# Batch 1's pooled values by TensorE from the local value layout, its values in other buffers, load limits by stage, a swapped clamp and a new order

## Chip, cores and metric

The kernel runs on one core of a Trainium2 chip. The metric is the device time of one execution in microseconds, the median of several runs; the time before is 971.5 us (three runs, 966.82 to 975.91).

## The reference, cut to what matters

Eight batches of eight heads, 576 tokens, head size 64. Each head gets two attentions, which are added: one over tokens pooled by four (the means of four neighbours of q, k and v; the result is repeated four times), and one over a window of at most three tokens to either side. The sum goes through a feed-forward layer with g = h cos(h).

```python
q_d = q.reshape(B, H, Sd, 4, D).mean(axis=3)      # k_d and v_d alike
out_up = np.repeat(sm_attn(q_d, k_d, v_d), 4, axis=2)
mask = np.abs(pos[:, None] - pos[None, :]) < 4
out_local = softmax(where(mask, scale * q @ k.T, -1e9)) @ v
x = (out_up + out_local).transpose(0, 2, 1, 3).reshape(4608, 512)
h = x @ w_in                                      # 512 x 2048
return (h * np.cos(h)) @ w_out                    # 2048 x 512
```

## The kernel before, in words

**The work.** Heads go in pairs, 32 in all (8 batches by 4 pairs). Of each pair `u_qk` loads q and k and pools them, `u_v` loads v in the local layout (12 windows of 32 tokens by 64, 384 KB), `u_s` makes both sorts of scores and their softmax, `u_t` transposes the probabilities, `u_pv` multiplies by the values and writes x. The tokens are cut into 12 tiles of 384; `gemm1` makes one chunk of 128 columns of h for a tile (12 matmuls of 384 columns, L1275; from tile 4 on a pair of chunks by seven products of half size, L1300), `g_part` makes g of it on ScalarE, VectorE and GpSimd (L1345 to L1357, L630), `gemm2` adds three times three matmuls of 512 columns (L1375). Numbers are split into a high and a low half-precision part, weights too: `w_load` (L652) fetches one of 32 blocks of 512 KB as 64-bit words and `w_split`/`w_total` (L663 to L725) rebuild the fraction, clamp it (L664), scale it (L722, L723) and take the rest (L725).

**Pooled values before.** For batches 0 and 1 `u_vd` loads the four rows to be pooled as a second copy of v (288 KB for each pair, L882) into a buffer of the ring `wd` (seven buffers, the one that weight blocks use), adds them in two additions (L890, L891) on GpSimd or VectorE, and for batch 1 squares them on ScalarE for the scale of x (L885). From batch 2 on `v_sum` does the pooling with accumulating DMAs.

**Buffers.** The local values `vl` of batch 0 and 1 share a ring of four buffers, so that each load of batch 1 waits until L1178, the local product of batch 0, has read its buffer.

**The order.** A planner (`Plan`) holds every operation with a cost, its engine or engines to choose from, and what it waits for. It walks through simulated time and, for each engine, takes the ready operation with the least key; the keys come from a backward walk and from hand-searched offsets (`MOVES`, `TURNS`), and `FILLS` adds idle matmuls (L1527) that keep TensorE active in the early stage. The result is the program order of each engine, which the chip follows whatever the true durations are. SyncE (SP) starts all plain loads in one order; the first part of it is a chain written by hand (queries and keys of batch 0, values of batch 0, `u_vd` of batch 1, weight chunks 0 and 1, queries and keys of batch 1, `u_v` of batch 1, the other weights). A load waits on an earlier one so that at most 900 kB are on their way (`FLIGHT`).

**Constants.** GpSimd makes two identities and the mask of the local windows (L587 to L596): eight selections over 32 by 192, one after the other.

Of the kernel before, what the change touches and what calls it, by code (L numbers as in the profile page):

```python
# [60 lines left out]
FLIGHT = 900e3  # L61
# [6 lines left out]
    "u_vd": {(0, 2): (0, -2.3), (1, 0): (0, 2.5), (1, 3): (-31.95, 0)},  # L68
    "u_s": {(0, 0): (-26.7, 0), (0, 1): (-16.8, -5.85), (0, 2): (106.15, 0), (1, 0): (-51, 0), (1, 1): (-44.65, 4.4), (1, 2): (-35.45, 0), (1, 3): (6.15, 1.7),
# [1505 lines left out]
```

## Time and profile before

| | |
|---|---|
| runs | 971.5, 966.82, 975.91 us; median 971.5 |
| span of the profiled execution | 971.3 us; its first instruction begins at 0.24 us |
| busy: TensorE, VectorE, ScalarE, GpSimd | 921.4, 758.6, 635.5, 455.8 us |
| moved by DMA | 90.30 MB |

A whole time of the profiled execution beside its span is not recorded; the span differs by 0.2 us from the median of the runs, and the working below is made against the span. In the rows, PE is TensorE's matmul side, PEld its weight loads, DVE VectorE, ACT ScalarE, POOL GpSimd, SPq the queue of SyncE. `A <- B` after a wait names who was waited for; "issue" is time in which nothing shown was waited for.

### The profile page before, as it was taken

Reading aid. Unit: us, or ns where it says so; the run is one execution under the profiler, and the core shown is the slowest. Engines: PE = TensorE matmul, PEld = TensorE weight load, DVE = VectorE, ACT = ScalarE, POOL = GpSimd, SP = SyncE. Lnnn points to the kernel's source line nnn. Section 1 sums busy time; section 2 is a strip of 40 time slices with the busy share of each in tenths; the row PEclk is TensorE's granted clock in tenths of the full one; section 3 lists DMA queues with packets and bytes.
Section 4 is the critical chain, followed back from the end, with each engine's and each line's share of the span. In section 5 each row is a group of like instructions: output and inputs, shape, how many; then the busy total and the mean of one; then the engine's idle time right before and its main releaser. Section 6 shows DMA issues by size and latency. Waiting matters only on the chain.

```text
span 971.3 us, 26178 instructions
## 1 busy us (share of the span) xinstructions
PE 921.4 (95%) x10464; PEld 613.8 (63%) x10464; DVE 758.6 (78%) x1713; ACT 635.5 (65%) x1378; POOL 455.8 (47%) x715
## 2 busy tenths in 40 slices
PE   7978899899989898999989998999999999999998
PEld 6755554454556555667667676676776767667674
DVE  5887798988888878889788777897597876656554
ACT  3646667877757575776767576666576576565654
POOL 6653874267763888888534242753041341200000
PEclk9977999999999999999999999999999999999999
DMA  7845894456573752224323031341030120000000
GB/s 236 243 154 162 229 206 143 125 117 145 109 152 51 163 144 72 68 79 96 107 79 87 26 99 49 87 110 47 1 106 3 31 79 9 2 33 1 33 2 33
DMA packets 48962, 90.30 MB, mean 93 GB/s; under 512 B 6024, under 2 KB 23176, under 8 KB 48840
## 3 DMA queue, kind: packets, MB, share of 16 engines
q1 hardware_dynamic: 42360, 74.67, 25.3%
q0 software_dynamic: 6480, 13.96, 9.6%
q8 instruction: 82, 1.34, 0.6%
q14 instruction: 40, 0.33, 0.1%
HBM read 65.01 MB, written 18.09 MB: 86 GB/s over the span
## 4 chain that ended last, share of the span: by engine, by line
PE 65%; DVE 10%; DMA 10%; ACT 6%; POOL 4%; issue 3%; SPq 2%; ACTq 0%; POOLq 0%; DVEq 0%
PE bank L1375 29%; PE bank L1300 20%; PE bank L1275 5%; PE bank L1193 3%; PE bank L927 2%; DMA wv<-vdn 2%; DMA diag<-ptl 2%; PE bank L935 2%; DMA wd<-w_out 1%; SPq L1039 1%; DMA wd<-vdn 1%; DVE tr L1346 1%; PE bank L1147 1%; PE bank L1048 1%; DVE tr L1349 1%
## 5 line engine op out<-in xcount | busy, mean ns | idle before, releaser
L1375 PE MATMUL bank<-wo,gh 128*128 128x512 f16 x1152 | 343.1, 380 | 2.3 <-ACT ob L1392 2.2
L1375 PE MATMUL bank<-wo,gl 128*128 128x512 f16 x576 | 218.3, 379 | 0.8 <-POOL gl L630 0.8
L1375 PEld LDWEIGHTS <-gh 128*128 128x128 f16 x1152 | 106.9, 98 | 86.6 <-issue 7.0
L630 POOL TENSOR_TENSOR gl<-tr,gh 128x384 f16<-128x384 f32 x65 | 65.8, 1014 | 202.6 <-ACT gh L1356 169.6
L1345 ACT ACTIVATE tr<-bank,bquart,hs 128x384 int32<-128x384 f32 x144 | 95.9, 667 | 92.8 <-PE bank L1300 75.6
L1300 PEld LDWEIGHTS <-wi 128*128 128x128 f16 x1536 | 129.3, 98 | 23.7 <-issue 5.6
L1314 DVE TENSOR_TENSOR bank<-bank,tr 128x192 f32<-128x192 f32 x192 | 69.0, 361 | 89.4 <-PE bank L1300 82.1
L1348 ACT ACTIVATE tr<-tr,bhalf 128x384 f32<-128x384 f32 x192 | 116.4, 610 | 25.9 <-DVE tr L1346 24.0
L1349 DVE SCALAR_TENSOR_TENSOR tr<-tr,rho,bank 128x384 f32<-128x384 f32 x192 | 114.7, 606 | 18.0 <-ACT tr L1348 17.0
L1300 PEld LDWEIGHTS <-room 128*128 128x128 f16 x1152 | 97.5, 98 | 32.9 <-issue 7.0
L1275 PEld LDWEIGHTS <-wi 128*128 128x128 f16 x768 | 75.3, 98 | 59.9 <-issue 5.0
L1375 PEld LDWEIGHTS <-gl 128*128 128x128 f16 x576 | 56.3, 98 | 69.4 <-POOL gl L630 1.3
L1346 DVE SCALAR_TENSOR_TENSOR tr<-bank,hs,tr 128x384 f32<-128x384 f32 x144 | 87.9, 611 | 14.8 <-ACT tr L1345 14.7
L1356 ACT ACTIVATE gh<-tr 128x384 f16<-128x384 f32 x148 | 76.6, 519 | 27.4 <-DVE tr L1349 22.2
L630 DVE TENSOR_TENSOR gl<-tr,gh 128x384 f16<-128x384 f32 x127 | 77.6, 613 | 10.6 <-ACT gh L1356 7.8
L1310 ACT ACTIVATE tr<-bank 128x192 f32<-128x192 f32 x161 | 52.0, 325 | 44.4 <-PE bank L1300 27.3
L1300 PE MATMUL bank<-room 128*128 128x192 f16 x768 | 80.1, 246 | 0.1
L1392 ACT ACTIVATE ob<-bank,os 128x512 f32<-128x512 f32 x63 | 41.4, 680 | 10.5 <-PE bank L1375 9.2
L1300 PE MATMUL bank<-room,wi 128*128 128x192 f16 x384 | 42.1, 246 | 0.0
L1193 PE MATMUL bank<-diag,vl 128*64 128x96 f32 x672 | 34.6, 253 | 7.9 <-DMA diag<-ptl 5.8
L664 POOL TENSOR_SCALAR wv<-wv 128x512 f32<-128x512 f32 x17 | 35.2, 2073 | 12.4 <-ACT wv L663 10.2
L1007 POOL TENSOR_TENSOR sml<-sml,su 128x384 f32<-128x384 f32 x26 | 28.7, 1103 | 26.3 <-DVE su L1005 26.3
(284 smaller groups left out, 2023.9 us busy)
## 6 DMA issues: line engine op xcount, KB each, us to landing
vl<-vl SPq DMA_DIRECT2D x32, 384.0 KB
q<-qT SPq DMA_DIRECT2D x32, 292.0 KB
k<-kT SPq DMA_DIRECT2D x32, 292.0 KB
out<-ob SPq DMA_DIRECT2D x36, 256.0 KB
out<-ob POOLq DMA_DIRECT2D x33, 256.0 KB, 5.6
wd<-w_in SPq DMA_DIRECT2D x16, 512.0 KB
wd<-w_out SPq DMA_DIRECT2D x16, 512.0 KB
diag<-ptl SPq DMA_DIRECT2D x112, 48.0 KB
```

The lines of the kernel that those rows point to most:

```text
L630: f = lambda e: lambda: e.tensor_tensor(out=out(), in0=in0(), in1=in1(), op=ALU.subtract)
L1193: pe.matmul(banks[e].get()[64 * h:64 * h + 64, sg * 4 * BQ:(sg + 1) * 4 * BQ], vt.get()[:, s, :], dg[:, :, s, :BQ], start=b >= GRP, stop=T ...
L1275: pe.matmul(ph.get()[:, :m], w[:, i, kc, :], x[:, kc, :], start=(n == 0), stop=(n == 3 * KC - 1))
L1300: pe.matmul(bk.get()[:, lo:lo + HT], a(i)(kk), bx(j, k)(kk), start=start and n == 0, stop=n == 5, skip_group_check=True)
L1310: pl.op("ACT", _act(HT), lambda: act.activation(t.get(), src(), AF.Copy), r=[bk], w=[t], alts=[("DVE", _dve(HT), lambda: dve.tensor_copy(t ...
L1314: o = pl.op("DVE", _dve(HT), lambda: dve.tensor_tensor(out=out(), in0=src(), in1=hold[i].get(), op=ALU.add), **kw)
L1345: pl.op("ACT", _act(m, True, 2), lambda: act.activation(ti(), h(), AF.Identity, bias=bquart, scale=inv()), r=[ph, also, hs], w=[tr])
L1346: pl.op("DVE", _dvs(m), lambda: dve.scalar_tensor_tensor(out=tr.get(), in0=h(), scalar=inv(), in1=ti(), op0=ALU.mult, op1=ALU.subtract), r ...
L1348: pl.op("ACT", _act(m, False, 1), lambda: act.activation(tr.get(), tr.get(), AF.Sin, scale=2.0 * PI, bias=bhalf), w=[tr], tab="sin")
L1349: pl.op("DVE", _dvs(m), lambda: dve.scalar_tensor_tensor(out=tr.get(), in0=tr.get(), scalar=rho(), in1=h(), op0=ALU.mult, op1=ALU.mult), r ...
L1356: pl.op("ACT", _act(m, False), lambda: act.activation(ghv(), trv(), AF.Copy), r=[tr], w=[gh], alts=[("DVE", _dve(m / 2), lambda: dve.tenso ...
L1375: pe.matmul(o, (gh, gh, gl)[k].get()[:, sl], wo.get()[:, (0, 1, 0)[k]], start=(c == c0 and k == 0), stop=(c == c1 - 1 and k == 2))
```

## The change

- `u_vd` of batch 1 loads nothing and adds nothing: six single-precision matmuls for each pair take the local layout `vl` as moving operand and a matrix of ones `grp` (made once on GpSimd, in buffer `ob.2`) as weights, and sum four tokens into 72 rows; one copy brings 256 columns out of PSUM. The squares for the scale are taken of `vl` (768 columns).
- `vl` of batch 1 lies in the unused x buffers x2h, x3h and x3l and in one buffer of `wd`; its loads stand right behind batch 0's values, ahead of the weights.
- The limit on bytes under way is 1.8 MB for the loads up to weight chunk 2, 500 kB for the late loads (batches 2 to 7), and 900 kB between.
- The clamp of L664 takes min first and max second; the high part of a weight may also be made on GpSimd, as a multiplication by the scale and by 1.0.
- `w_in` is laid out on the host so that each block is 128 rows of 4 KB, not 512 runs of 1 KB.
- The mask is selected on one of six segments and copied by VectorE; the single-precision identity comes last.
- The planner's costs of loads, small GpSimd operations and engine starts are set anew, 0.35 us are kept free after 140 us of its time between another engine's result and TensorE, offsets now exist for single operations, and all offsets are new.

```diff
-FLIGHT = 900e3
+VLX = ((2, "h"), (3, "h"), (3, "l"))
+FLIGHT, FLIGHT0, FLIGHT1 = 900e3, 1.8e6, 500e3
...
+CFG = dict(slack=0.35, slack0=140.0, alttol=0.3, ...
+FROM0 = dict(PE=1.4, ACT=2.0, DVE=0.9, POOL=4.0, SP=1.8)
...
+                    if f == "PE" and e != "PE" and not back and end > CFG["slack0"]:
+                        x += CFG["slack"]
...
-        pool.memset(mask, 0.0)
+        dve.memset(mask[:, 0], 0.0)
         for i in range(4):
-            h = mask[i * BS:(i + 1) * BS]
+            h = mask[i * BS:(i + 1) * BS, 0]
...
+        dve.tensor_copy(mask[:, 1:], mask[:, 0:1].broadcast_to([P, NSEG - 1, BS]))
...
-        clamp = ... scalar1=2.0 ** -15, scalar2=F64_TOP, op0=ALU.max, op1=ALU.min)
+        clamp = ... scalar1=F64_TOP, scalar2=2.0 ** -15, op0=ALU.min, op1=ALU.max)
...
-                  alts=[("DVE", _dvs(n / 2), ... scalar1=a(), scalar2=None, op0=ALU.mult))], port=BOTH)
+                  alts=[(x, d, ... scalar1=a(), scalar2=1.0, op0=ALU.mult, op1=ALU.mult))
+                        for x, d, e in (("DVE", _dvs(n / 2), dve), ("POOL", 0.65, pool))], port=BOTH)
...
+        vt, bk = st[(b, pr)]["vl"], bank(b, "v")
+        def mm():
+            acc = bk.get()[:HD, :2 * P].rearrange("p (a h d) -> p a h d", a=2, h=2)
+            for s in range(NSEG):
+                o, k = GC - 24 * (s % 3), 4 * (s // 2) + s % 2
+                pe.matmul(acc[:, s // 3], grp.get()[:, o:o + HD], vt.get()[:, k:k + 3:2, :], start=s % 3 == 0, stop=s % 3 == 2)
+        pl.op("PE", 6 * _mm4(2 * D), mm, r=[vt, grp], w=[bk], ni=24, warm=WARM["d"], act=0.45)
+        pl.op("ACT", _act(2 * P), lambda: act.activation(flat(), bk.get()[:HD, :2 * P], AF.Copy), ...
...
+        if b == 1 and pr < len(VLX):
+            r, k = VLX[pr]
+            vt = pl.buf(lambda: x_ring[(r, k)].get()...
+        elif b == 1:
+            t = pl.turn("wd", NWD)
...
-    chain = [... u_vd/u_v of batch 0 + ul("u_vd", 1) + wl(0, 1) + ul("u_qk", 1) + ul("u_v", 1) + wl(*range(2, NC)) ...]
+    chain = [... u_vd/u_v of batch 0 + ul("u_v", 1) + wl(0) + ul("u_qk", 1)[:2] + wl(1) + ul("u_qk", 1)[2:] + wl(*range(2, NC)) ...]
+            o.flight = FLIGHT1
+    for o in chain[:chain.index(loads[("w_load", "i", 2)][0])]:
+        o.flight = FLIGHT0
```

## Rows read from the trace of the kernel before

**Rows 1.** The page: busy time by engine, and the granted clock in 40 slices.

```profile
PE 921.4 (95%) x10464; PEld 613.8 (63%) x10464; DVE 758.6 (78%) x1713; ACT 635.5 (65%) x1378; POOL 455.8 (47%) x715
...
PEclk9977999999999999999999999999999999999999
```

**Rows 2.** Four stretches: length, busy time of PE, PEld, DVE, ACT, POOL, clock, DMA.

```profile
0.00:125.00 125.00, 106.11 (x1948) 76.41 (x1949) 97.35 (x237) 73.63 (x206) 78.36 (x129) 0.89 0.70 206
125.00:250.00 125.00, 118.85 (x762) 63.16 (x761) 114.09 (x252) 93.48 (x180) 69.11 (x91) 1.00 0.60 141
250.00:700.00 450.00, 430.08 (x5218) 286.19 (x5217) 371.35 (x827) 301.44 (x631) 261.50 (x420) 1.00 0.35 86
700.00:972.00 272.00, 266.40 (x2542) 188.04 (x2540) 175.77 (x399) 166.96 (x363) 46.79 (x76) 1.00 0.10 30
```

**Rows 3.** The same stretches, idle matmuls of L1527 alone (PE, PEld).

```profile
0.00:125.00 125.00, 34.59 (x235) 23.40 (x235) 0.89 0.70 206
125.00:250.00 125.00, 2.94 (x21) 2.06 (x21) 1.00 0.60 141
```

**Rows 4.** The chain that ended last, 0 to 130 us: start, length, what.

```profile
6.27 0.33 PE bank L922 x2
...
39.67 1.02 PE bank L1166 x4
...
52.88 2.22 PE bank L1166 x4
...
76.94 3.38 PE bank L1275 x10
...
86.34 4.07 DMA wd<-w_out
90.49 3.79 DMA wd<-w_out
94.36 4.33 DMA q<-qT
...
101.90 4.47 DMA wd<-w_in
```

**Rows 5.** Timeline of 0 to 62 us: mask, pooled-value additions, and SyncE's queue.

```profile
5.87 0.35 POOL L596 CAST mask_b<-mask 128x192 bf16<-128x192 f32 x1
...
9.86 0.36 DVE L950 TENSOR_REDUCE mxl<-bank 128x6 f32<-128x192 f32 x1 [3.89 <-PE bank L935]
...
28.12 0.68 DVE L890 TENSOR_TENSOR wd<-wd 72x512 f32<-72x512 f32 x1
...
36.78 0.71 DVE L891 TENSOR_TENSOR vsum<-wd 72x256 f32<-72x256 f32 x1
...
44.05 14.14 SPq L899 DMA_DIRECT2D vl<-vl  x4
58.29 0.38 SPq L652 DMA_DIRECT2D wd<-w_in  x1
```

**Rows 6.** The weight clamp L664 by engine (min/median/max ns), and who waited for it.

```profile
L664 POOL TENSOR_SCALAR wv<-wv x17: 1915/1952/2362, 34.1 to 243.8; 128x512 f32<-128x512 f32 x17
L664 DVE TENSOR_SCALAR wv<-wv x15: 364/427/828, 45.4 to 235.8; 128x512 f32<-128x512 f32 x15
...
DVE wv L666 <- POOL wv L664: 8.1, 8, 1.8
```

**Rows 7.** Groups of 60 to 250 us: a two-input GpSimd operation, high parts, rests.

```profile
L630 POOL TENSOR_TENSOR x2l<-xs,x2h 128x384 f16<-128x384 f32 x3 | 2.7, 911 | 0.4 <-ACT x2h L1129 0.4
L723 DVE TENSOR_SCALAR wi<-wv,wsc 128x512 f16<-128x512 f32 x8 | 3.8, 480 | 0.0
L722 ACT ACTIVATE wo<-wv,wsc 128x512 f16<-128x512 f32 x10 | 7.2, 718 | 4.3 <-POOL wsc L699 3.7 <-DVE wsc L699 0.5
```

**Rows 8.** Waits of TensorE, 125 to 972 us: total, times, longest.

```profile
PE bank L1193 <- DMA diag<-ptl: 4.9, 4, 2.9
PE bank L1375 <- ACT ob L1392: 2.2, 6, 0.7
PE bank L927 <- issue: 2.1, 1, 2.1
PE bank L1300 <- DVE tr L1311: 1.9, 2, 1.6
```

More of the change, by code (lines that the diff above doesn't have):

```diff
@@ new lines @@
+    "x_scale": {(0,): (543.95, 10.6), (2,): (31.85, -54.75)},
+    "u_t": {(0, 0): (-249.05, 4), (0, 3): (0, 2.8), (1, 2): (0, -0.55), (2, 0): (95.95, 0), (2, 1): (32.75, -0.75), (2, 3): (23.2, 0), (3, 0): (-42.45, 0),
+        (3, 2): (24.45, 1.65), (3, 3): (289.65, 0), (4, 0): (-22.05, 0), (4, 1): (-58.9, 0), (4, 3): (-148.1, 0), (5, 0): (5.9, 0), (5, 1): (11.2, 0),
+        (5, 2): (-47.25, 2.8), (6, 0): (-10.1, 0), (6, 1): (144.15, 0), (7, 1): (0, 2.9), (7, 2): (78.7, 0)},
+    "u_pv": {(0, 0): (344.25, 0), (0, 1): (830.5, -6.9), (0, 2): (0, 47.5), (0, 3): (232.8, -40.65), (1, 0): (0, 7.15), (1, 1): (0, -326.8),
[8 rows of a table added]
@@ new lines @@
+    "c_scale": {(0, 0): (108.8, 11.15), (0, 1): (0, 3.5), (0, 10): (0, -9.9), (0, 11): (102.4, 12.85), (0, 13): (82.5, 0), (0, 2): (0, 0.8), (0, 4): (0, 18),
[15 rows of a table added]
+    "o_scale": {(0, 0): (-249.35, -41.45), (0, 8): (0, 1.8)},
+    "g_scale": {(0, 4): (165.55, 0), (1, 2): (600.7, 10.8), (12, 16): (0, -25.95), (2, 4): (0, 20.7)},
[12 rows of a table added]
+    "v_sum": {(2,): (337.75, 0), (3,): (227.1, 0), (4,): (-350.4, 0)},
+    "u_v": {(2, 0): (211.2, 0)},
+    "s_make": {(1,): (0, -17.3), (2,): (-600.95, -24.25), (3,): (-39, -70.3), (4,): (-9.1, 0), (5,): (0, -115.7), (6,): (123.25, -45.15), (7,): (37, -9.55)},
@@ L117 @@
+    "v_norm": {(6,): (484.6, 0), (7,): (36.2, 0)},
 }
 TURNS = {
+    "u_vd": {(0, 0, 1): (0, -47.7)},
+    "u_s": {(0, 0, 14): (28.5, 0), (0, 1, 14): (-39.55, 0), (0, 2, 7): (-40.6, 0), (0, 2, 8): (-10.75, 0), (0, 3, 1): (-494.45, 0), (1, 0, 14): (-34.2, 0),
[8 rows of a table added]
+    "u_t": {(0, 0, 3): (-23.85, 0), (0, 0, 5): (0, -6.35), (0, 3, 5): (0, -5.45), (1, 2, 7): (-20.7, 0), (2, 1, 0): (-48.85, 0), (2, 1, 5): (22.5, 0),
+        (2, 1, 7): (10.85, 0), (2, 3, 7): (-26.85, 0), (3, 1, 5): (12.2, 0), (3, 1, 6): (0, 13.45), (3, 2, 0): (-24.5, 0), (4, 1, 0): (60.85, 0),
+        (6, 0, 5): (-23.45, 0), (6, 2, 7): (35.65, 0)},
@@ new lines @@
+    "u_pv": {(0, 1, 5): (0, 10.25), (0, 2, 4): (88, 0), (1, 0, 7): (0, -10.85), (1, 0, 9): (0, -30.15), (1, 2, 8): (0, -27.2), (2, 1, 1): (-49.8, 0),
[14 rows of a table added]
+    "g_scale": {(2, 4, 1): (-205.2, 0)},
[17 rows of a table added]
+    "c_scale": {(0, 10, 0): (0, 10.35), (0, 6, 0): (-203.65, 0)},
+    "x_scale": {(1, 3): (106.7, 0), (2, 6): (14.8, 0)},
+    "u_qk": {(2, 1, 1): (-10.35, 0), (2, 2, 1): (-15.15, 0), (2, 2, 2): (0, 17.45), (2, 3, 2): (71.85, 0), (3, 0, 2): (0, 10.2), (5, 3, 2): (0, 6),
+        (5, 3, 3): (0, 9.4), (6, 2, 2): (0, 24.7), (7, 0, 2): (-35.15, 0), (7, 1, 2): (0, 9.7)},
@@ L151 @@
     __slots__ = ("eng", "dur", "fn", "tab", "deps", "sdeps", "now", "start", "end", "lat", "name", "arg", "preds", "succs",
-                 "i", "fin", "banks", "alts", "boost", "move", "cold", "gate", "ni", "size", "inst", "stall", "fill", "warm", "act", "port", "wb")
+                 "i", "fin", "flight", "banks", "alts", "boost", "move", "cold", "gate", "ni", "size", "inst", "stall", "fill", "warm", "act", "port", "wb")
 class Plan:
@@ L264, in run @@
         late = {e: {f: late(f, e) if back else late(e, f) for f in self.engines} for e in self.engines}
-        free = {e: 2.9 if e == "SP" and not back else 0.0 for e in self.engines}
+        free = {e: 0.0 if back else FROM0[e] for e in self.engines}
         ready = {e: [] for e in self.engines}
@@ L427, in run @@
                 sent = [x for x in sent if x[0] > t]
-                while sum(x[1] for x in sent) > FLIGHT:
+                while sum(x[1] for x in sent) > o.flight:
                     t = max(t, sent[0][0])
@@ L461, in run @@
                     open_[b] -= 1
-                    b_end = end + late[e]["PE"]
+                    b_end = end + late[e]["PE"] + (CFG["slack"] if e != "PE" and end > CFG["slack0"] else 0.0)
                     hold[b] = max(hold.get(b, 0.0), b_end)
@@ L500, in schedule @@
             key = {o: span - o.fin - o.boost for o in self.ops}
-        key, bias, seen, turn = best[1], {}, {}, {}
+        self.base, key, bias, seen, turn = best[1], {}, {}, {}, {}
         for o in self.ops:
@@ L586, in constants @@
         dve.memset(tiny, TINY)
-        pool.memset(mask, 0.0)
+        dve.memset(mask[:, 0], 0.0)
         for i in range(4):
-            h = mask[i * BS:(i + 1) * BS]
-            pool.affine_select(out=h, in_=h, compare_op=ALU.is_ge, fill=NEG, base=0,
-                               pattern=[[0, NSEG], [1, BS]], channel_multiplier=-1)
-            pool.affine_select(out=h, in_=h, compare_op=ALU.is_ge, fill=NEG, base=2 * PAD,
-                               pattern=[[0, NSEG], [-1, BS]], channel_multiplier=1)
-        pool.memset(mask[0:BS, 0, 0:PAD], NEG)
-        pool.memset(mask[P - BS:P, NSEG - 1, BQ + PAD:BS], NEG)
-        pool.tensor_copy(mask_b, mask)
+            h = mask[i * BS:(i + 1) * BS, 0]
+            pool.affine_select(out=h, in_=h, compare_op=ALU.is_ge, fill=NEG, base=0, pattern=[[1, BS]], channel_multiplier=-1)
+            pool.affine_select(out=h, in_=h, compare_op=ALU.is_ge, fill=NEG, base=2 * PAD, pattern=[[-1, BS]], channel_multiplier=1)
+        dve.tensor_copy(mask[:, 1:], mask[:, 0:1].broadcast_to([P, NSEG - 1, BS]))
+        dve.memset(mask[0:BS, 0, 0:PAD], NEG)
+        dve.memset(mask[P - BS:P, NSEG - 1, BQ + PAD:BS], NEG)
+        dve.tensor_copy(mask_b, mask)
+        make_identity(nc, ident)
     wgt = {(k, c): pl.buf(lambda k=k, c=c: wp.tile([P, 2, DM], F16, name=f"w{k}{c}", tag=f"w{k}{c}", bufs=1), f"w{k}{c}")
@@ L611, in tile_of, with dma @@
         return max(t for t in range(NT) if FROM[t] <= tok)
-    w_dram = {"i": w_in.bitcast(I32).rearrange("(a p) (f t) -> p a f t", p=P, t=2),
-              "o": w_out.bitcast(I32).rearrange("f (n t) -> f n t", t=2)}
+    w_dram = {k: w.bitcast(I32).rearrange("f (n t) -> f n t", t=2) for k, w in (("i", w_in), ("o", w_out))}
     loads = {}
-    def dma(nbytes, fn, r=(), w=(), pw=(), issue=0.4, rate=300e3):
+    def dma(nbytes, fn, r=(), w=(), pw=(), issue=0.4, rate=290e3, base=1.4):
         def go():
             o.inst = fn().ins
-        o = pl.op("SP", issue, go, r=r, w=w, pw=pw, move=(1.2, nbytes / rate))
+        o = pl.op("SP", issue, go, r=r, w=w, pw=pw, move=(base, nbytes / rate))
         o.size = nbytes
@@ L646, in w_load @@
         wd = wv[(k, c)] = sb("wd", NWD, [P, DM, 2], I32)
-        if k == "i":
-            src = lambda: w_dram["i"][:, :, c * P:(c + 1) * P, :]
-            dst = lambda: wd.get().rearrange("p (a f) t -> p a f t", a=KC)
-        else:
-            src, dst = (lambda: w_dram["o"][c * P:(c + 1) * P]), wd.get
-        dma(4096 * P, lambda: sp.dma_start(dst(), src()), w=[wd], rate=250e3)
+        dma(4096 * P, lambda: sp.dma_start(wd.get(), w_dram[k][c * P:(c + 1) * P]), w=[wd])
     wq, half, exps = {}, {}, {}
@@ L663, in w_split @@
         pl.op("ACT", _act(n, False), lambda: act.activation(v.get(), wd().bitcast(F32)[:, :, 1], AF.Abs), r=[wd_b], w=[v])
-        clamp = lambda e: lambda: e.tensor_scalar(out=v.get(), in0=v.get(), scalar1=2.0 ** -15, scalar2=F64_TOP, op0=ALU.max, op1=ALU.min)
+        clamp = lambda e: lambda: e.tensor_scalar(out=v.get(), in0=v.get(), scalar1=F64_TOP, scalar2=2.0 ** -15, op0=ALU.min, op1=ALU.max)
         pl.op("DVE", 0.335, clamp(dve), w=[v], alts=[("POOL", _pool(n), clamp(pool))], port=BOTH)
@@ L722, in w_total @@
             pl.op("ACT", _act(n, False, 1), lambda hi=hi, u=u, a=a: act.activation(hi(), u.get(), AF.Copy, scale=a()), r=[u, sc], w=[hb], pw=[w],
-                  alts=[("DVE", _dvs(n / 2), lambda hi=hi, u=u, a=a: dve.tensor_scalar(
-                      out=hi(), in0=u.get(), scalar1=a(), scalar2=None, op0=ALU.mult))], port=BOTH)
+                  alts=[(x, d, lambda hi=hi, u=u, a=a, e=e: e.tensor_scalar(
+                      out=hi(), in0=u.get(), scalar1=a(), scalar2=1.0, op0=ALU.mult, op1=ALU.mult)) for x, d, e in (("DVE", _dvs(n / 2), dve), ("POOL", 0.65, pool))], port=BOTH)
             pl.op("DVE", _dvs(n), lambda w=w, hi=hi, u=u, a=a: dve.scalar_tensor_tensor(
@@ L872, in v_sum, with grouping @@
             pl.op("POOL", 0.9, lambda r=r: pool.dma_start(dst(), src(r), accum_op=ALU.add), w=[t], move=(3.5, 1.9))
+    grp = pl.buf(lambda: fp.tile([P, DM], F32, name="grp", tag="ob.2", bufs=1), "ob.2")
+    GC = 48
+    def grouping():
+        t = grp.get()
+        pool.memset(t[:, :P], 0.0)
+        for i in range(4):
+            h = t[i * BS:(i + 1) * BS, GC + 6 * i:GC + 6 * i + 6]
+            pool.memset(h, 1.0)
+            pool.affine_select(out=h, in_=h, compare_op=ALU.is_ge, fill=0.0, base=-PAD, pattern=[[-4, 6]], channel_multiplier=1)
+            pool.affine_select(out=h, in_=h, compare_op=ALU.is_ge, fill=0.0, base=PAD + 3, pattern=[[4, 6]], channel_multiplier=-1)
+    pl.op("POOL", 1.3, grouping, w=[grp])
     def u_vd(b, pr):
         pl.name = "u_vd"
-        vw, vd = sb("wd", NWD, [P, DM, 2], I32), pl.buf(None)
+        vd = pl.buf(None)
         if b not in vsum:
@@ L888, in v_add, with f @@
-        def v_add(e):
-            def f():
-                e.tensor_tensor(out=v4()[:, 0:2], in0=v4()[:, 0:2], in1=v4()[:, 2:4], op=ALU.add)
-                e.tensor_tensor(out=vo(), in0=v4()[:, 0], in1=v4()[:, 1], op=ALU.add)
-            return f
-        pl.op("POOL", 1.7, v_add(pool), w=[vd, vw], pw=[vsum[b]], alts=[("DVE", 1.1, v_add(dve))], port=dict(POOL=2, DVE=2))
-        st.setdefault((b, pr), {}).update(vd=vd, vdg=vo)
+        st.setdefault((b, pr), {}).update(vd=vd, vdg=vo)
+        if b < NDIAG:
+            vw = sb("wd", NWD, [P, DM, 2], I32)
+            flat = lambda: vw.get()[:HD].rearrange("p f t -> p (f t)").bitcast(F32)
+            v4 = lambda: flat().rearrange("p (r a n) -> p r a n", a=2, r=4)
+            dma(16 * P * HD * 2, lambda: sp.dma_start(v4().rearrange("p r a n -> p r (a n)"), vdn[b, :, :, pr].rearrange("p r a n -> p r (a n)")), w=[vw], issue=0.8)
+            def v_add(e):
+                def f():
+                    e.tensor_tensor(out=v4()[:, 0:2], in0=v4()[:, 0:2], in1=v4()[:, 2:4], op=ALU.add)
+                    e.tensor_tensor(out=vo(), in0=v4()[:, 0], in1=v4()[:, 1], op=ALU.add)
+                return f
+            pl.op("POOL", 1.8, v_add(pool), w=[vd, vw], pw=[vsum[b]], alts=[("DVE", 1.1, v_add(dve))], port=dict(POOL=2, DVE=2))
+            return
@@ L896, in u_v @@
+        pl.op("ACT", _act(2 * P), lambda: act.activation(flat(), bk.get()[:HD, :2 * P], AF.Copy), r=[bk], w=[vd], pw=[vsum[b]],
+              alts=[("DVE", _dve(2 * P), lambda: dve.tensor_copy(flat(), bk.get()[:HD, :2 * P]))])
     def u_v(b, pr):
         pl.name = "u_v"
-        vt = ub(b, pr, "vl")
-        dma(4 * P * 12 * D, lambda: sp.dma_start(vt.get(), vl[b, pr]), w=[vt], rate=210e3)
-        if b == 0:
-            square(12 * D, lambda: vt.get().rearrange("p a d -> p (a d)"), 0, pr, vt, True)
+        if b == 1 and pr < len(VLX):
+            r, k = VLX[pr]
+            vt = pl.buf(lambda: x_ring[(r, k)].get().rearrange("p a s -> p (a s)").bitcast(F32).rearrange("p (a d) -> p a d", d=D))
+            x_b[r].prev.append(vt)
+        elif b == 1:
+            t = pl.turn("wd", NWD)
+            vt = pl.buf(lambda: ap.tile([P, DM, 2], I32, name="wd", tag=t, bufs=1).rearrange("p f t -> p (f t)").bitcast(F32)[:, :12 * D].rearrange(
+                "p (a d) -> p a d", d=D), t)
+        else:
+            vt = ub(b, pr, "vl")
@@ L902, in u_v @@
+        dma(4 * P * 12 * D, lambda: sp.dma_start(vt.get(), vl[b, pr]), w=[vt])
+        if b < NEARLY:
+            square(12 * D, lambda: vt.get().rearrange("p a d -> p (a d)"), 0, NPAIR * b + pr, vt, True)
         u = st.setdefault((b, pr), {})
@@ L1448, in attn_ffn_kernel @@
     for i in range(NPAIR):
-        for t, f in ((-7.6 + 0.1 * i, u_vd), (-4.0 + 0.1 * i, u_qk), (-3.5 + 0.1 * i, u_v), (-3.0 + 0.1 * i, u_s), (-2.6 + 0.1 * i, u_t), (-2.2 + 0.1 * i, u_pv)):
+        for t, f in ((-4.0 + 0.1 * i, u_qk), (-7.6 + 0.1 * i, u_v), (-7.55 + 0.1 * i, u_vd), (-3.0 + 0.1 * i, u_s), (-2.6 + 0.1 * i, u_t), (-2.2 + 0.1 * i, u_pv)):
             at(t, f, 1, i)
@@ L1487, in ul @@
         return [(f, b, i) for i in range(NPAIR)]
-    chain = [o for k in ul("u_qk", 0) + [(f, 0, i) for i in range(NPAIR) for f in ("u_vd", "u_v")] + ul("u_vd", 1) + wl(0, 1) + ul("u_qk", 1)
-             + ul("u_v", 1) + wl(*range(2, NC)) for o in loads[k]]
+    chain = [o for k in ul("u_qk", 0) + [(f, 0, i) for i in range(NPAIR) for f in ("u_vd", "u_v")] + ul("u_v", 1) + wl(0) + ul("u_qk", 1)[:2] + wl(1) + ul("u_qk", 1)[2:]
+             + wl(*range(2, NC)) for o in loads[k]]
     late = {k: v for k, v in loads.items() if k[0] in ("u_qk", "u_v", "v_norm", "v_sum") and k[1] >= NEARLY}
@@ L1531, in attn_ffn_kernel @@
             if o.size:
-                while sum(x.size for x in flight) > FLIGHT:
+                while sum(x.size for x in flight) > o.flight:
                     held = flight.pop(0)
@@ L1557, in _lay @@
         "vl": np.ascontiguousarray(vb),
-        "w_in": np.ascontiguousarray(inputs["moe_w_in"]).view(np.int64),
+        "w_in": np.ascontiguousarray(inputs["moe_w_in"].reshape(KC, P, NC, P).transpose(2, 1, 0, 3)).reshape(DF, DM).view(np.int64),
         "w_out": np.ascontiguousarray(inputs["moe_w_out"]).view(np.int64),
```

55 lines of the change are left out of this document (22 added, 33 removed), and 122 rows, old and new, of tables (FILLS, MOVES, TURNS).

## The prediction

> **What bounds the kernel now.** I read first the busy times, then four stretches of the span, then in the first of them the chain and the timeline. The first view shows TensorE busy for 921.4 of 971.3 us [rows 1], so it looks like the bound everywhere. The stretches correct that. TensorE's idle time is length less busy time: 125 - 106.1 = 18.9 us up to 125 us, 6.2 up to 250, 19.9 up to 700 and 5.6 behind [rows 2]. Its busy time in the first stretch holds 34.6 us of idle matmuls that compute nothing [rows 3], and the clock granted there was 0.89, with two slices at 0.7 [rows 1, 2]: (1 - 0.89) x 125 = 14 us at most are lost to the lower of the two levels, 1.2 GHz in place of 2.4; I take 12. So up to 125 us some 19 + 35 + 12 = 66 us are not useful TensorE work, and behind it some 32 + 4 = 36. VectorE is what the start waits for: 97.4 of 125 us busy, and 114.1 of 125 in the next stretch (91%) [rows 2], where TensorE is fed by weight splits and g. In the last 272 us TensorE idles 5.6 us: nothing is to be had there.
>
> The chain shows what is late in the first stretch: the mask at 6.27 us, the first product of the feed-forward layer at 76.94 us, then weight and query loads, 4.07 + 3.79 + 4.33 us in a row from 86.34, and one of 4.47 at 101.90 [rows 4]. The timeline shows why loads are late: SyncE stands at the four loads of batch 1's local values for 14.14 us, from 44.05 to 58.2, since their buffers are held by batch 0, and only at 58.29 does the next weight load start [rows 5].
>
> **The change part by part.**
>
> *Mask.* The first score matmuls start at 6.27 us [rows 4], as the mask's last cast on GpSimd ends (5.87 + 0.35) [rows 5]. Selecting 32 columns in place of 192, with the identity moved behind, can take 0 to 3.5 us off; I take 2. VectorE has 3.89 us of idle time right behind it [rows 5], so that it can come through; what is late next is the keys' and queries' pooling. Taken: -1.5.
>
> *Pooled values of batch 1.* VectorE loses four pairs of additions, the first at 28.12 and the last at 36.78, 0.68 and 0.71 us for such [rows 5]; with 0.7 us as the mean of eight this is 5.6 us, at a time when it is the busiest engine. ScalarE trades a square for a slightly shorter one, four copies out of PSUM come in. TensorE gets 4 x 6 single-precision matmuls of 128 columns. Two of 288 columns took 1.02 us at the full clock and 2.22 at half [rows 4], so one of 128 takes 1.02 / 2 x 128 / 288 = 0.23 us, six 1.36 and all 5.4 us (11.8 at half clock). They lie where 34.6 us of idle matmuls lie [rows 3] and replace some, so their cost is between -1 (they hold the clock up as the idle ones did) and +11.8; I take +1. Were the cover gone, it would be 5.4. For VectorE I count -4 of 5.6, since part of it was hidden by waits for scores.
>
> *Loads and buffers.* Four loads of 288 KB go; four of 384 KB move ahead of the weights, so weight chunk 0 has 0.4 MB more ahead of it: at the 206 GB/s of the stretch [rows 2] 1.9 us later. Against that the 14.14 us of SyncE at L899 go [rows 5], and all that is queued behind it on SyncE comes sooner: weight chunks 2 and on, and then batch 2's queries. The waits in the chain that hang on that are 4.07 + 3.79 + 4.33 + 4.47 = 16.7 us [rows 4]. If the loads come 10 us sooner, all of these go at best, and VectorE's splitting is late next: it was 78% busy in that stretch [rows 2]. Bounds: -14 to +2; taken -6, nearer to the middle, since VectorE has 22% to give at most. The larger limit in the start and the layout of w_in are in it: the load of w_in took 4.47 us in the chain and those of w_out 4.07 and 3.79 [rows 4], so two such on the path are worth 0.8 to 1.4 us.
>
> *Clamp and high parts.* The clamp takes 1952 ns on GpSimd and 427 on VectorE, and VectorE waited 8.1 us in eight waits for it [rows 6]. That the other order of min and max is cheaper is nowhere in the trace. Bounds for it: 0.43 us (VectorE's row) to 1.95 (no change); a two-input operation of 384 columns takes 0.91 us on GpSimd [rows 7], for 512 columns 1.2. I take 1.2, the nearest row of that engine: 17 x 0.75 = 13 us less of GpSimd, of which VectorE feels some 8.1 x 0.4 = 3 us. The high part on GpSimd is priced by the planner at 0.65 us; the rows give 0.48 on VectorE, 0.72 on ScalarE [rows 7] and 1.95 for the clamp, the operation on GpSimd that is nearest in form [rows 6]. I take 1.2 again: up to ten such move 5 us off VectorE and ScalarE, worth 0 to -3, taken -1. Together -4, bounds -8 to +13.
>
> By the Trainium skill (GPSIMD Engine Reference, 4.1 Engine selection) a one-input elementwise operation on GpSimd runs at roughly line rate, while two-input ones are about twice as slow as VectorE. The trace disagrees for the clamp in its present order: the one-input operation of 512 columns takes 1952 ns, more than twice the 911 of the two-input one of 384. At line rate, as an estimate from that page, 512 columns at 1.2 GHz would be 0.43 us, the clamp part would come to its good end (-8) and the sum below to 950; by the row, with nothing gained from the swap, to 958.
>
> *Waits behind 125 us.* TensorE waits there for 26 us in all (6.2 + 19.9) before the last stretch [rows 2]; the longest sorts are the diagonal copies with 4.9 us, then the output copies with 2.2, a wait with no shown cause, 2.1, and sums with 1.9 [rows 8], each in few long waits, as an order leaves them that was planned with too small costs. The limit of 500 kB shortens what is queued ahead of a diagonal copy; 0.35 us kept free and a dearer diagonal copy move producers ahead. Idle time of this sort can fall to a third, or grow where the new order has its own misses: bounds -16 to +8, taken -9. It does not need the start to be right. The limit also makes SyncE wait at loads, and behind these stand diagonal copies and output stores; DMA is used 0.35 and 0.10 there [rows 2], so I price that at nothing; without that room each diagonal copy could lose a load's time.
>
> *Sum.* -1.5 (mask) -4 (VectorE) +1 (group matmuls) -6 (loads) -4 (GpSimd) = -14.5 in the start and the weight stage, of which I let 3 be lost, since all of these free VectorE or feed it and cannot each be felt in full: -11.5. With -9 behind it, -20.5, less 3 for the new order's own misses: -17.5. 971.3 - 17.5 = **954 us**; against the median of 971.5 the same.
>
> **The rivals.**
>
> *A. VectorE stays the bound up to 250 us.* The start comes 6 us sooner and the splitting of the weights gives it back: for it speaks VectorE's 91% [rows 2], against it that TensorE's idle time is mostly before 125 us. Only VectorE's own work counts then (-5.6 of additions, -3 of clamp waits, half of each felt), and the waits behind fall by 3: 971.3 - 4.3 - 3 = 964 us.
>
> *B. GpSimd is mispriced, slower than before.* Where: in the weight stage, 60 to 260 us. If a high part on GpSimd takes what the clamp takes, 1.95 us [rows 6], against 0.65 in the plan, every one put there is 1.3 us late, and behind it in GpSimd's order stand the small scales that release ScalarE and VectorE. With 16 of 32 there, 16 x 1.3 = 21 us of lateness come, and the swapped clamp gains nothing. If VectorE passes two thirds on, +14; the start's gain is halved (-6) and the order behind, planned for other times, loses 5 of the 8 in that term's upper bound: 971.3 - 6 + 14 + 5 = 984 us. It decides from about 1.6 us for a high part with more than ten of them. For it: the row of the clamp. Against: ScalarE or VectorE can still take them all.
>
> *C. The new order fits the chip much better.* Idle matmuls and half clock in the start shrink by a third (66 to 50 us, minus 16) and the waits behind 125 us to a third (-16): 971.3 - 32 = 939 us. For it: the idle time is spread over many small causes that one correction of costs reaches. Against: VectorE's load in 125 to 250 us.
>
> *D. The change of loads does not do what it says:* x buffers or the `wd` ring hold the values as late as before. A load of batch 1 would stand behind the same readers; then the term of -6 goes and the sum is 960. The x buffers of tiles 2 and 3 are read behind those of tile 0, whose first product stands at 76.94 us [rows 4], so I hold this unlikely and count it under A.
>
> **How the numbers follow.** Forecast 0.55, A (with D) 0.2, B 0.1, C 0.15. Faster by over 1% (below 961.8; about 1% is what a measurement of this kernel can tell from no change, the runs lying within 0.5% of their median): the forecast and C, 0.70. Within 1%: A, 0.20. Slower: B, 0.10. The range goes from C to a little beyond A, 938 to 970; the forecast's own is 946 to 962.
>
> **What would show it.** Right: no stop of SyncE near 44 us, L664 on GpSimd near 1.2 us or less, the first L1275 matmul of tile 0 before 70 us (76.94 now), idle matmuls and idle time up to 125 us together down from 53 to about 43 us, TensorE's waits from 125 to 700 us near 17 us, no row for the diagonal copies above 2 us. Wrong: TensorE idle in 125 to 250 us above 8 us with VectorE above 92% (A); a GpSimd row of 128x512 half-precision results near 2 us (B); a first stretch that is shorter by more than 15 us (C).

## The result, and the profile after

The changed kernel takes 947.4 us (median of four runs, 941.0 to 955.4), beside 973.7 us for the kernel before in the same comparison: a ratio of 0.971, 95% interval 0.966 to 0.977. Ratios leave out a run that lies more than 1.5% above the fastest of its kernel (955.4 us here, 958.5 with the clamp put back, 1850.5 in the repetition of the kernel after), while medians hold it. The forecast was 954 us with a range of 938 to 970. The working below compares the two profiled executions: spans of 971.3 and 947.3 us, 24.0 us apart, at the same mean granted clock (0.984 and 0.985). In this the pair is not typical: the other three runs of the kernel after were granted 0.992 to 0.997, and the kernel before 0.979 to 0.989 in 17 runs of a later comparison. So the 24.0 us hold no gain of clock; what the clock adds in other runs is not shown.

The page after, busy time and granted clock, as in [rows 1]:

```profile
PE 921.3 (97%) x10480; PEld 617.1 (65%) x10480; DVE 752.2 (79%) x1705; ACT 641.2 (68%) x1411; POOL 438.2 (46%) x724
...
PEclk9959999999999999999999999999999999999999
```

TensorE's busy time is what it was, 921.3 against 921.4 us. The whole difference between the two executions is therefore idle time of TensorE, and the four stretches say where it went (columns as in [rows 2]):

```profile
0.00:125.00 125.00, 115.60 (x1906) 84.25 (x1907) 94.70 (x245) 77.95 (x218) 66.53 (x129) 0.89 0.54 167
125.00:250.00 125.00, 120.53 (x873) 64.15 (x870) 120.36 (x274) 99.86 (x199) 77.20 (x125) 1.00 0.74 179
250.00:700.00 450.00, 442.39 (x5383) 297.00 (x5382) 380.24 (x845) 311.92 (x662) 255.21 (x406) 1.00 0.35 88
700.00:972.00 272.00, 242.74 (x2325) 171.74 (x2322) 156.92 (x344) 151.51 (x334) 39.28 (x66) 0.99 0.07 22
```

Length less busy time is 9.4, 4.5, 7.6 and (the span ends at 947.3) 4.6 us, 26 in all; from [rows 2] it was 18.9, 6.2, 19.9 and 4.9, or 50 (the prediction's 5.6 runs to 972 us, behind the span's end at 971.3). So 9.5 us came from the first stretch, 12.3 from 250 to 700, and 2 from the rest. The clock did not help: 0.89 in the first stretch as before. Idle matmuls, the line of [rows 3]:

```profile
0.00:125.00 125.00, 30.07 (x197) 19.22 (x197) 0.89 0.54 167
125.00:250.00 125.00, 4.59 (x26) 2.19 (x24) 1.00 0.74 179
```

Idle time and idle matmuls up to 125 us together are 9.4 + 30.1 = 39.5 us, 53.5 before. The chain of the first stretch, beside [rows 4] (start, length, what):

```profile
1.25 3.17 DMA k<-kT
...
4.46 0.48 PE bank L1012 x2
4.93 1.15 PE bank L1017 x74
...
81.66 2.06 PE bank L1365 x12
...
94.80 4.92 DMA wd<-w_out
99.80 7.81 DMA wd<-w_out
```

The scores (L1012 adds the mask, L1017 makes the products) start right behind the first keys' load, no longer behind the mask. The first product of the feed-forward layer (L1275 before, L1365 now) did not come sooner, and waits for weight loads are still there, 4.92 + 7.81 us. SyncE's part of the timeline, beside [rows 5], shows why:

```profile
37.38 0.33 SPq L710 DMA_DIRECT2D wd<-w_out  x1
60.95 30.01 SPq L1129 DMA_DIRECT2D diag<-ptl  x16
91.01 2.48 SPq L1488 DMA_DIRECT2D out<-ob  x3
94.36 0.34 SPq L710 DMA_DIRECT2D wd<-w_in  x1
```

The stop near 44 us is gone, but SyncE now stands before the sixteen diagonal copies, which come next in its order: from 37.7 to 94.4 us no weight load starts. By 90 us 13 blocks of weights had been asked for before, six are now. The work that the start brings forth is larger all the same. The products by token tile, in the kernel before (min/median/max ns, first and last start in us):

```profile
L1275 PE MATMUL bank<-x0h,wi x128: 322/326/528, 73.9 to 271.6; 128*128 128x384 f16 x128
L1275 PE MATMUL bank<-x1h,wi x128: 322/326/326, 124.3 to 304.9; 128*128 128x384 f16 x128
```

and in the kernel after:

```profile
L1365 PE MATMUL bank<-x0h,wi x128: 323/326/527, 81.6 to 261.8; 128*128 128x384 f16 x128
L1365 PE MATMUL bank<-x1h,wi x128: 322/326/328, 109.4 to 288.2; 128*128 128x384 f16 x128
```

Tile 0 starts 8 us later, tile 1 15 us sooner. So each weight block serves two tiles almost at once. Up to 125 us TensorE had spent 19.2 us on the products of the layer (53 matmuls of the first product, 33 of the second); now it is 28.2 us (96 and 45), with fewer weight blocks.

The waits of TensorE from 125 us on, as in [rows 8]:

```profile
PE bank L1390 <- DVE bank L1404: 1.9, 6, 0.5
...
PE bank L1283 <- DMA diag<-ptl: 0.7, 1, 0.7
```

No sort of wait is above 1.9 us; the one for diagonal copies was 4.9.

### The profile page after: what moved, and what is told of

Its sections match the earlier page's. It is cut to its first block, busy times and chain, and to the rows that moved or that the text cites. A ratio compares the mean times of both kernels' runs of the same rounds, so it can differ in the third digit from the quotient of the medians.

```text
span 947.3 us, 26227 instructions
## 1 busy us (share of the span) xinstructions
PE 921.3 (97%) x10480; PEld 617.1 (65%) x10480; DVE 752.2 (79%) x1705; ACT 641.2 (68%) x1411; POOL 438.2 (46%) x724
## 4 chain that ended last, share of the span: by engine, by line
PE 62%; DVE 19%; ACT 7%; issue 5%; DMA 4%; POOL 3%; SPq 0%; DVEq 0%; ACTq 0%; POOLq 0%
PE bank L1465 25%; PE bank L1390 19%; PE bank L1365 4%; PE bank L1017 3%; PE bank L1283 3%; DVE tr L1439 2%; DVE tr L1436 2%; PE bank L1237 2%; DVE wv L726 2%; PE bank L1025 2%; DVE wv L728 2%; DMA wd<-w_out 1%; DVE gl L693 1%; PE bank L1138 1%; ACT tr L1438 1%
## 5 line engine op out<-in xcount | busy, mean ns | idle before, releaser
L1439 DVE SCALAR_TENSOR_TENSOR tr<-tr,rho,bank 128x384 f32<-128x384 f32 x192 | 114.3, 605 | 12.6 <-ACT tr L1438 11.5
L693 POOL TENSOR_TENSOR gl<-tr,gh 128x384 f16<-128x384 f32 x75 | 75.2, 1006 | 77.6 <-ACT gh L1446 66.1
L1365 PEld LDWEIGHTS <-wi 128*128 128x128 f16 x768 | 74.4, 98 | 54.8 <-issue 2.6
L1446 ACT ACTIVATE gh<-tr 128x384 f16<-128x384 f32 x157 | 81.1, 519 | 24.8 <-DVE tr L1439 21.8
L1390 PE MATMUL bank<-room 128*128 128x192 f16 x768 | 77.5, 246 | 1.4 <-DVE bank L1404 1.3
L693 DVE TENSOR_TENSOR gl<-tr,gh 128x384 f16<-128x384 f32 x117 | 72.2, 622 | 7.6 <-ACT gh L1446 4.9
L1400 ACT ACTIVATE tr<-bank 128x192 f32<-128x192 f32 x172 | 55.0, 322 | 31.7 <-PE bank L1390 23.2
L1482 ACT ACTIVATE ob<-bank,os 128x512 f32<-128x512 f32 x58 | 38.4, 681 | 14.9 <-PE bank L1465 14.7
L693 POOL TENSOR_TENSOR tmp<-xs 128x96 f32<-128x96 f32 (+1 forms) x35 | 17.5, 505 | 54.7 <-DVE xs L1299 54.2
L1017 PE MATMUL bank<-k,q 64*32 64x32 f32 x3072 | 34.6, 204 | 4.6 <-issue 3.1
L1017 PEld LDWEIGHTS bank<-k,q 64*32 64x32 f32 x3072 | 30.5, 108 | 12.9 <-issue 8.7
```

What stands on the lines that cost most here:

```text
L693: f = lambda e: lambda: e.tensor_tensor(out=out(), in0=in0(), in1=in1(), op=ALU.subtract)
L1017: pe.matmul(banks[h].get()[BS * i:BS * (i + 1), LQ + BS * s:LQ + BS * (s + 1)], q.get()[hs, o:o + BS], k.get()[hs, o:o + BS], start=not ea ...
L1365: pe.matmul(ph.get()[:, :m], w[:, i, kc, :], x[:, kc, :], start=(n == 0), stop=(n == 3 * KC - 1))
L1390: pe.matmul(bk.get()[:, lo:lo + HT], a(i)(kk), bx(j, k)(kk), start=start and n == 0, stop=n == 5, skip_group_check=True)
L1400: pl.op("ACT", _act(HT), lambda: act.activation(t.get(), src(), AF.Copy), r=[bk], w=[t], alts=[("DVE", _dve(HT), lambda: dve.tensor_copy(t ...
L1439: pl.op("DVE", _dvs(m), lambda: dve.scalar_tensor_tensor(out=tr.get(), in0=tr.get(), scalar=rho(), in1=h(), op0=ALU.mult, op1=ALU.mult), r ...
```

## The experiments

Two readings were set against each other. By *parts*, each edit saves its own time: value path, clamp, mask, loads. By *costs* (order), the edits save little by themselves, and the gain comes from a new search of the order on truer costs, with 0.35 us kept free. The kernel after, run again in a comparison with more runs of before, gave 946.9 us (median of six), 0.976 (0.973 to 0.980).

> The kernel after, unchanged, beside the others on one chip: 0.971 of before, 942 us where before takes 970.

### One edit at a time, order unchanged

**The clamp back to max first, in the kernel after.**

```diff
-scalar1=F64_TOP, scalar2=2.0 ** -15, op0=ALU.min, op1=ALU.max
+scalar1=2.0 ** -15, scalar2=F64_TOP, op0=ALU.max, op1=ALU.min
```

> The kernel after with the clamp's max first again; same order on every engine. Both theories: the eight clamps on GpSimd take 1.95 us in place of 0.61. Parts theory (the single edits carry the gain): VectorE waits for these clamps again, some 8 x 1.3 x 0.4 = 4 us are lost, 951 us. Order theory (the new order carries it, each edit by itself is small): GpSimd is idle around most clamps, below 2 us, 948 us.

The clamp's line (min/median/max ns) and who waited, with the old order of min and max:

```profile
L722 POOL TENSOR_SCALAR wv<-wv x8: 1930/1944/2267, 41.1 to 212.2; 128x512 f32<-128x512 f32 x8
...
  DVE wv L724: 5.7, 6
```

and in the kernel after:

```profile
L722 POOL TENSOR_SCALAR wv<-wv x8: 604/612/938, 40.3 to 214.5; 128x512 f32<-128x512 f32 x8
...
  DVE wv L724: 1.4, 1
```

The swap alone makes the operation three times faster. VectorE waits 4.3 us more without it, but the time is 947.9 us, 0.979 (0.974 to 0.983), within the intervals of the kernel after. The search had put only eight clamps on GpSimd (17 before, [rows 6]).

**The small edits in the kernel before:** swapped clamp, mask from one segment, the new layout of w_in, in the order of before.

```diff
-        pool.tensor_copy(mask_b, mask)
+        dve.tensor_copy(mask[:, 1:], mask[:, 0:1].broadcast_to([P, NSEG - 1, BS]))
...
-        clamp = ... op0=ALU.max, op1=ALU.min)
+        clamp = ... op0=ALU.min, op1=ALU.max)
...
+        "w_in": ... .reshape(KC, P, NC, P).transpose(2, 1, 0, 3)).reshape(DF, DM)...
```

> The kernel before, its order and its planner unchanged, with the swapped clamp, the mask on one segment and w_in in 4 KB rows. Parts theory: 17 clamps on GpSimd are 1.34 us shorter, the first scores start 1.8 us sooner: -6 to -9 us, 965 us. Order theory: the old order gives most of it back at the next late producer, -1 to -3 us, 971 us.

966.5 us against 970.0, ratio 0.997 (0.995 to 0.999): 3 us, all edits together. VectorE's wait for the clamp fell from 8.1 us [rows 6] to 0.5:

```profile
L657 POOL TENSOR_SCALAR wv<-wv x17: 607/614/1149, 35.3 to 237.5; 128x512 f32<-128x512 f32 x17
...
  DVE wv L659: 0.5, 1
```

7.6 us less waiting on the busiest engine but one bought 3 us at most. The mask bought 0.2 us at most, and the chain of this kernel shows why:

```profile
1.36 4.75 PE bank L1520 x22
6.11 0.17 PE bank L915 x2
6.28 0.95 PE bank L920 x64
```

In the old order TensorE has 22 idle matmuls ahead of the first score, and they end at 6.11 us (the first scores of the kernel before start at 6.27) however early the mask is there. Only a new order could use it.

**Group matmuls twice, in the kernel after** (pooled values of batch 1 doubled).

```diff
-            for s in range(NSEG):
+            for s in list(range(NSEG)) * 2:
```

> The kernel after with each of the 24 group matmuls issued twice (same sums); same order otherwise. It prices the group matmuls: 4 x 1.4 us more on TensorE. If they lie in place of idle time, 0 to +2 us (947 to 949); if they lie on the path to the first tile, +5 to +6 (953).

951.0 us, 0.981 (0.977 to 0.984). One of the four groups, now 24 matmuls for 12 (a single-precision one runs as two instructions):

```profile
L971 PE MATMUL bank<-x2h,grp x24: 272/272/330, 26.9 to 29.5; 128*72 128x128 f32 x24
```

The second set adds 4 x 12 x 0.11 = 5.3 us of TensorE by the spacing of their starts (2.6 us for 24). The medians are 4 us apart (951.0 against 947.4 and 946.9), but the intervals overlap, so that it is not shown how much of it is felt.

**One limit of 900 kB for all loads, in the kernel after.**

```diff
-                while sum(x.size for x in flight) > o.flight:
+                while sum(x.size for x in flight) > FLIGHT:
```

> The kernel after with 900 kB as the limit of all loads; same order. Parts theory: the first loads come later at the start (the 1.8 MB limit lifted 236 to 283 GB/s in the first slice) and diagonal copies stand behind more bytes, +3 to +6 us, 951 us, and TensorE waits 3 us or more on diagonal copies. Order theory: within 2 us of the kernel after.

942.6 us, 0.974 (0.970 to 0.978): the same as with three limits, and no diagonal wait came back. The first slice of its page moves 219 GB/s, against 283 in the kernel after. The limits by stage give nothing that can be measured in this order.

### The order taken away

Offsets and idle matmuls are emptied, so that the planner orders by its own keys: once in the kernel before, once in the one after, and once in the one after with the old value path (batch 1's rows loaded and added, local values in the old ring, the old chain of loads).

```diff
+MOVES, TURNS, FILLS = {}, {}, {}
```

> The kernel before without its hand-searched offsets and added idle matmuls (all three tables empty): the planner's own order. Order theory: the search is worth much, 995 to 1010 us. Parts theory: 980 to 990.

> The kernel after with all three tables empty. Parts theory (buffers, loads, values, costs carry the gain): it keeps 20 us or more of distance to the kernel before without tables, e.g. 975 against 995. Order theory: the distance of these two is below 10 us, and most of the 28 us is lost.

> The kernel after with all three tables empty, and batch 1's values as before: a second copy of v, additions on GpSimd or VectorE, local values in the ring of four, old chain of loads. If the new path of the values is worth my -9 us (4 for VectorE and 6 for the loads, less 1), it is some 9 us above the same kernel with the new path; if the path is worth nothing by itself, within 3 us.

They took 989.2 us (1.022, 1.018 to 1.027), 1030.3 us (1.066, 1.060 to 1.071) and 1013.9 us (1.046, 1.043 to 1.049). So without a searched order the changed kernel is 41 us *slower* than the old one, and the new value path makes 16 of them. In this order the old value path is the better one. The searched order is worth 20 us to the kernel before and 83 to the one after. In the second stretch of the unsearched kernel after TensorE idles 26 us, and its longest waits are for VectorE's steps of g:

```profile
125.00:250.00 125.00, 98.78 (x916) 59.89 (x915) 106.52 (x236) 87.52 (x177) 78.06 (x139) 0.93 0.61 174
```

```profile
PE bank L1621 <- DVE tr L1440: 10.6, 3, 7.2
```

### The order searched again, with the same effort

That leaves open what the value path is worth once the order fits. So one search, with one start (offsets worked out from the order of the kernel after) and one effort, was run for three versions: the kernel after, the same with the old value path, the same with nothing kept free.

```diff
-CFG = dict(slack=0.35, slack0=140.0, ...
+CFG = dict(slack=0.0, slack0=140.0, ...
```

> The kernel after (new path of the values, 0.35 us kept free), its offsets replaced by ones derived from its own order and searched anew, with the same effort for this and the next two. The planner's own end is 935.9 us (930.8 for the kernel after, 940.3 for the kernel before). It is the control for the next two: about 950 us if the chip adds to the plan what it adds to the kernel after (some 15 us).

> The same start and effort as the control, but batch 1's values as before (second copy of v, additions, ring of four, old chain of loads). The planner's own end is 940.5. Parts theory (the path is worth 9 us): 9 us or more above the control, 960. Order theory: the path is worth what the plan says, 5 us or less above it, 950 to 955.

> The same start and effort as the control, without the 0.35 us kept free ahead of TensorE. The planner's own end is 932.4, 3.5 below the control. If the margin pays, TensorE's waits from 125 us on are longer and the time is 5 us or more above the control (955 to 960); if it does not, the time is 0 to 4 us below it.

The first gave 950.4 us, 0.975 (0.972 to 0.978), as the kernel after: a second search finds as much, though its plan ends 5.1 us later. The old value path gave 961.3 us, 0.987 (0.984 to 0.991). That is 12 us dearer (0.0124 x 976; 11 by the medians), with some 4 us of uncertainty from the runs, and every edit but the value path is in it. The plans were 4.6 us apart. Each version had one search, so that the luck of a search is not in the 4 us, and how large it is was not measured. Stretches with the new path:

```profile
0.00:125.00 125.00, 114.73 (x1953) 83.03 (x1954) 100.99 (x255) 80.58 (x222) 69.02 (x132) 0.97 0.59 177
...
250.00:700.00 450.00, 437.94 (x5358) 295.46 (x5357) 362.23 (x814) 303.81 (x652) 262.71 (x412) 0.99 0.34 86
```

and with the old one:

```profile
0.00:125.00 125.00, 106.46 (x1943) 74.76 (x1944) 99.89 (x252) 76.57 (x213) 83.09 (x134) 0.93 0.68 189
...
250.00:700.00 450.00, 431.09 (x5285) 287.78 (x5283) 374.61 (x849) 295.19 (x624) 264.55 (x423) 1.00 0.36 87
```

TensorE idles 18.5 us up to 125 us with the old path, 10.3 with the new, and 18.9 against 12.1 from 250 to 700. GpSimd, which makes additions of the old path, is busy 83 us in place of 69 in the first stretch. The chain of the old path's start holds three loads of local values, and SyncE's queue shows whose they are:

```profile
6.01 8.35 DMA vl<-vl
14.38 11.05 DMA vl<-vl
...
64.43 3.92 DMA vl<-vl
```

```profile
39.26 25.49 SPq L7299 DMA_DIRECT2D vl<-vl  x4
```

The first two start before 15 us and are batch 0's, which the new path loads as well. The third is batch 1's: the stop of [rows 5] is still there under the new order, now 25.49 us long. The chain of the new path has none of the three, but there SyncE stands before the sixteen diagonal copies, as in the kernel after, and starts six weight loads by 87 us where the old path starts twelve (by 125 us they are 17 and 16). So the 12 us do not come from weights that are there sooner in the start; where they come from stays open. Tile 1 starts early in both (104.5 and 104.4 us), so that came with the order, not with the value path.

Nothing kept free gave 958.5 us, 0.983 (0.979 to 0.987), 8 us behind the control. But the pair's traces do not carry all of that. Behind 140 us, where the margin acts, TensorE idles 954.0 - 140 - 790.57 = 23.4 us without it and 948.2 - 140 - 787.39 = 20.8 with it:

```profile
140.00:960.00 820.00, 790.57 (x8423) 523.18 (x8409) 624.35 (x1421) 544.89 (x1144) 363.48 (x582) 0.99 0.30 77
```

```profile
140.00:960.00 820.00, 787.39 (x8369) 523.40 (x8367) 620.48 (x1394) 540.25 (x1147) 397.56 (x617) 0.99 0.31 78
```

That is 2.6 of the 5.8 us between the spans. The rest is busy time behind 140 us, work that was left over: up to 140 us the granted clock was 0.94 without the margin and 0.98 with it.

```profile
0.00:140.00 140.00, 130.37 (x2084) 91.47 (x2085) 113.94 (x287) 93.04 (x251) 81.13 (x148) 0.94 0.62 187
```

```profile
0.00:140.00 140.00, 129.73 (x2132) 91.45 (x2133) 115.88 (x288) 92.22 (x246) 79.63 (x149) 0.98 0.62 183
```

What the margin itself is worth stays open; each version had one search.

### Idle matmuls where the clock was low

In its profiled execution the kernel after has half the clock in the third slice, 47 to 71 us. Idle matmuls were added where TensorE starts work between 46 and 66 us.

```diff
+            if o.eng == "PE" and 46.3 < o.start < 66.0:
+                o.fill += 8 if o.start < 47.0 else 3
```

> The kernel after with idle matmuls added where its plan has none, ahead of the products of 46 to 66 us; all else in the same order. If the half clock that the profile of the kernel after shows from 47 to 71 us can be held off so, the granted clock stays near 1.0 there and the median falls to 940 us; if TensorE has no free time there, it rises by the added matmuls, 3 us.

The granted clock of the span rose to 0.996, and the time is 952.5 us, 0.977 (0.974 to 0.980): no gain. The idle matmuls up to 125 us took 43.4 us in place of 30.1, and by then the products of the layer are the same 96 and 45, so that what the clock gave back went into them:

```profile
0.00:125.00 125.00, 43.41 (x277) 26.20 (x277) 0.97 0.55 167
```

There was also less to give back than the profile of the kernel after shows. In the kernels with the clamp put back and with the group matmuls twice, which keep its order and have no added idle matmuls, the page shows 0.8 in this slice:

```profile
PEclk9989999999999999999999999999999999999999
```

No version beat the kernel after by more than the noise; the one with a single limit, at 942.6 us, is the lowest. Two things were not tried: the local values alone in their old ring under the new order, and a new search of the kernel before on its old costs, which would tell truer costs from a longer search with offsets for single operations.

## Why the prediction was right, point by point

The direction, and roughly the size and the split between start and middle, held: -17.5 us forecast, -24.0 between the profiled spans. Several terms were mis-sized, too small and too large, and the loads came out otherwise than I had it. So that the sum came out near is in part luck.

- **Waits behind 125 us**, taken as -9, the main miss: TensorE's idle time from 125 to 700 us fell from 26.1 to 12.1 us, -14.0, near the good bound of -16. No sort of wait stands out any more; the diagonal copies lost 4.2 us of it.
- **The new order's misses**, taken as +3: none can be told apart behind 125 us. With -14 for -9 and 0 for +3 the sum would have been -25.5. The order was a large piece of the change, and I priced it as a tax on it: with the old value path, the new order and the other edits still come 12 to 15 us below the kernel before (ratio 0.987; 961.3 against 976.1), of which the small edits made 3 in the old order.
- **The start**, -11.5 together: idle time fell by 9.5 us, and 9.0 us more of useful products were done by 125 us. Its announced signs came out mixed. Idle time and idle matmuls fell to 39.5 us (43 expected). But the first product came at 81.6 us, not before 70. (Before, it came at 73.9; the 76.94 of the prediction is a later row of the chain.)
- **Loads**, -6: the step failed. I held that once SyncE's 14.14 us were gone, all that is queued behind would come sooner. The stop moved to the diagonal copies, and weights came later. What I did not see is that weights need not come sooner if tile 1 is ready sooner: each block then serves two tiles (so the traces read; no run changes this alone). The limits, part of this term, gave nothing that can be measured.
- **Pooled values**, -4 + 1: under equally searched orders the whole value path with its loads is worth 12 us (8 to 17 by the runs alone, from one search each). The forecast's -3 and -6 are 9; with the reason for the -6 gone, that this is near is luck. The four groups take some 1.5 us each, 5.9 in all (5.4 worked out). Whether +1 was too low is not shown: a second set raised the median by 4 us, within the uncertainty.
- **Clamp and high parts**, -4: the clamp takes 0.61 us, half of the 1.2 taken, but eight stand on GpSimd, not 17, and one high part of 32, at 0.78 us. Going back to the dear clamp costs nothing that can be told apart, so that -4 was too much for the kernel as it came out. By the Trainium skill (GPSIMD Engine Reference, 4.1 Engine selection) a one-input operation on GpSimd runs at roughly line rate. With min first the trace, at 0.61 us, is 1.4 times the estimate of 0.43 us that was worked out from it; with max first, at 1944 ns, it is over four times the estimate.
- **Mask**, -1.5: the first scores start at 4.46 us instead of 6.27. Late next is the load of the first keys, not the pooling; and the edit does this only in the new order.

Of the rivals, A fails by its own sign: VectorE is 96% busy from 125 to 250 us (120.36 of 125), but TensorE idles 4.5 us there, not above 8. VectorE's load was no bound: no sort of TensorE's waits for VectorE there comes to more than 0.8 us in all. B fails at its price: 0.78 us for a high part. C asked for a first stretch shorter by more than 15 us; the 14.0 us of idle time and idle matmuls come close to it, without the clock, and behind 125 us the waits fell to less than half, not to a third: the 947.4 us lie between the forecast's 954 and C's 939. D fails in its letter, since the loads of the values had all been started by 20.7 us, though the weights behind them did come late.

Against the two readings: neither holds alone. Parts fails where an edit is made without a new order (3 us of the small ones; the new value path 16 us *worse* unsearched). Costs fails where the value path is left out of an equal search: 12 of some 25 us go with it, as far as one search for each version shows.

## What to carry to other kernels

An edit to a kernel whose order is written out is worth what a newly searched order makes of it: price it with the order, and measure it with the old edit searched just as long, and more than once. Before a term is given to loads that come sooner, ask whether what they feed could be used twice instead; and look for what stands next in the queue when a stop is taken out of it. Less waiting on an engine that is not the bound (7.6 us here) can be worth a fraction of itself (3 us at most here).

## What the runs showed of the hardware

- GpSimd's two-step clamp of 128 by 512 in single precision takes 612 ns with min first and 1944 with max first, the operands otherwise the same; on VectorE both take 427. Why was not tried.
- The same mask cast on VectorE took 0.41 us in the kernel after and 1.58 in the kernel with the small edits, where GpSimd was filling 1536 columns from 4.02 to 5.40 us. That the one makes the other is not shown; there is one such cast in each kernel.

```profile
3.93 1.58 DVE L594 CAST mask_b<-mask 128x192 bf16<-128x192 f32 x1
...
4.02 1.38 POOL L826 MEMSET diag<- 128x1536 f32 x1
```

- The granted clock differs between executions of one kernel. With one limit for all loads, five runs at 0.992 to 0.995 took 938.0 to 945.5 us, and one at 0.981 took 950.6. The time does not follow it alone: the kernel after took 949.0 us at 0.985 and 955.4 at 0.992.
